# Cosformer attention into a GEGLU block on one core: another order for batch 0's opening, and batch 1's last 64 positions and a GpSimd copy in a later place

## The chip, the core and the metric

The kernel runs on one core of a Trainium2 chip. The core has a matrix engine (TensorE, PE in the profile; PEld is its loading of weights), a vector engine (VectorE, DVE), a scalar engine (ScalarE, ACT), GpSimd (POOL) and SyncE (SP), which here issues most of the DMA transfers. Each engine runs its instructions in the order in which the program issues them, and they wait for each other by semaphores. PSUM, the matrix engine's output memory, has eight banks of 512 fp32 columns for each of 128 partitions. The metric is the time of one execution on the device, in microseconds; lower is better.

## The reference

Eight batches of eight heads, 576 positions and 64 values per head go through a linear attention. Its result, as rows of 512 values, goes through a feed-forward block with a gate.

```python
batch, n_heads, seq, head_dim = (8, 8, 576, 64)
theta = pi / 2 * arange(S) / S
phi(x) = concatenate([relu(x) * cos(theta), relu(x) * sin(theta)], axis=-1)   # 64 -> 128 features
q_p, k_p = phi(q), phi(k)
kv  = einsum('bhsf,bhsd->bhfd', k_p, v)
z   = sum(k_p, axis=2)
num = einsum('bhsf,bhfd->bhsd', q_p, kv)
den = einsum('bhsf,bhf->bhs', q_p, z)[..., None] + 1e-06
x   = (num / den) as rows of tokens: 4608 x 512

g   = x @ w_gate                       # 512 x 1536
val = x @ w_val                        # 512 x 1536
out = (gelu(g) * val) @ w_out          # 1536 x 512
```

## The kernel before

**Attention.** The 576 positions of a batch lie in five tiles: tiles 0 to 3 have 128 positions, tile 4 the last 64. `load` (L76) brings a tensor of one batch in two DMAs, for the odd and the even partitions; `h0:h1` picks heads and `j0:j1` tiles. `sq` and `sk` (L351, L354) multiply one tile of q or k by cosine or sine and apply relu, on DVE (`"v"`) or ACT (`"s"`). `cast_v` (L140) casts heads of v to bf16, beside a column of ones. `kv_heads` (L152) multiplies keys by values, 5 matmuls a head, into one bank for four heads, and `kv_evac` (L166) copies that bank to SBUF; `kv_half` does both. q is turned either by PE (`q_by_pe`, L323, 8 transposes into a bank, with a copy `q_evac`, L331) or by a DMA on SP (`turn_q`, L144). `numer_mm` (L171) multiplies turned queries by kv, four matmuls for each group of four heads; `norm` (L180) adds epsilon (den), takes the reciprocal (rec) and multiplies (xb), all on DVE. The result, in one of four rotating buffers `xb`, is turned into `xT`, either by PE (`x_by_pe`, L339, with a copy) or by a DMA transpose on SP (`turn_x`, L204). For tile 4 that DMA writes a buffer `xr`, and a POOL copy (L212) brings 64 columns of it into `xT`.

**Feed-forward.** It runs in nine blocks: block 0 has the 576 tokens of batch 0, blocks 1 to 7 have 512 tokens each and block 8 has 448, so from block 1 on a block doesn't end where a batch does; the last 64 positions of batch 1 belong to block 2. A block has 12 units, one for each 128 columns of the 1536. In a unit, `gate` (L217) makes 4 matmuls into a bank and ACT applies Gelu into `gel`; `value` (L228) makes 4 matmuls into another bank, and DVE multiplies `gel` by it into `hT`. `o_part` (L259) makes 12 matmuls per 128 tokens for the output projection; ACT copies the bank to `o_sb`, and SP stores it. `hT` has two tiles, used by turns. Output tiles are aligned to 128 tokens of the whole sequence, so the last 64 tokens of a block go along with the next one: `carry(n)` (L245), one POOL copy of 12 x 64 columns from one `hT` to the first 64 columns of the other.

**Order.** All is written out by hand: instructions go to each engine in program order. `dummies` (L126) are matmuls on zeros whose results nobody reads.

- L86 to L103: loads of batch 0, on SP and one on ACT: k in two halves; q's first two tiles; v as heads 0 to 3, 4 and 5, 6 and 7; q's other tiles.
- L358 to L399: the opening: k scaled, q's tiles 0 and 1 scaled and turned by PE, v cast, kv made and copied, tiles 0 and 1 of the attention of batch 0. L363 and L398 are tiny copies that make POOL's weight loads (`load_w`, L307) wait: the first for q's first tiles, the other for x0.
- L413 to L448: block 0 by pieces. Its gates and values for units 0 to 5 are mixed with tiles 2, 3 and 4 of batch 0's attention. `Y(t, bank)` is the numerator and norm of tile t into that bank and the next; `X(t, bank, eng)` turns it into `xT`. `gv_unit(n, jt, c0, w, gb, vb, mid)` is a gate into bank gb, the steps of `mid`, then the value into bank vb; A is columns 0 to 255 and Bw 256 to 575.
- L451 to L456: q of batch 1 and w_out on POOL's queue; a tiny POOL copy (L454) that waits for a w_out load; behind it k and v of batch 1 on SP.
- L466 to L482: the rest of block 0's units; the table `between` puts q of batch 1 and, after unit 11, `carry(0)` among them.
- L483 to L522: k and v of batch 1, its kv, and tiles 0 to 3 of its attention, among the output tiles of block 0.
- From L524: `attn_step(b, i)`: for i = 0 the keys by values of batch b into banks 6 and 7, with copies; for i > 0 tile i-1 into `bank` and the next, turned by SP. `mid[n][jt]` holds steps that run between gate and value of unit jt of block n, `after[n][jt]` those that run behind the unit. For block 1, `attn_step(2, 0)` stands in `after[1][4]`, `attn_step(2, 1)` (banks 6 and 7) in `after[1][5]`, and `attn_step(2, 2)` (banks 4 and 5) in `mid[1][6]`. `attn_step(1, 5)`, batch 1's tile 4, stands in `mid[1][3]`.

Of the kernel before, what the change touches and what calls it, by code (L numbers as in the profile page):

```python
# [16 lines left out]
def kernel(  # L17
# [44 lines left out]
    vf = sb.tile([128, H, NJ + 1, D], FP32, name="vf")  # L62
# [13 lines left out]
    def load(dst, t, b, h0=0, h1=H, even=None, odd=None, j0=0, j1=NJ + 1):  # L76
        runs = t[b, h0:h1].rearrange("h (i r) d -> i h r d", r=9)
        for s, r0, n, eng in ((1, 5, 4, odd), (0, 0, 5, even)):
            n = min(n, j1)
            (eng or nc.sync).dma_start(  # L80
                out=dst[s:128:2, h0:h1, j0:n].rearrange("p h j d -> p h (j d)"),
                in_=runs[:, :, r0 + j0:r0 + n].rearrange("i h r d -> i h (r d)"),
            )
# [14 lines left out]
    nc.gpsimd.memset(vf[:, :, NJ], 0.0)  # L98
    load(qf, q, 0, j1=2)
    load(vf, v, 0, 0, 4)  # L100
    load(vf, v, 0, 4, 6)
    load(vf, v, 0, 6, 8)
    load(qf, q, 0, j0=2)  # L103

    nc.vector.tensor_scalar(par_i, par_i, 1, None, op0=ALU.bitwise_and)  # L105
# [20 lines left out]
    def dummies(n, bank=7):  # L126
        for _ in range(n):
            nc.tensor.matmul(ps[:, bank, :], lhsT=junk[:, 0:128], rhs=junk, start=True, stop=True)  # L128
# [11 lines left out]
    def cast_v(b, h0, h1, eng="v"):  # L140
        cp = nc.vector.tensor_copy if eng == "v" else nc.scalar.copy
        cp(vx[b % 2][:, :, h0:h1, 0:D], vf[:, h0:h1].rearrange("p h j d -> p j h d"))  # L142
# [6 lines left out]
        )  # L149


    def kv_heads(b, h0, h1, bank):  # L152
        for h in range(h0, h1):
            for j in range(NJ + 1):
                nc.tensor.matmul(  # L155
                    ps[:, bank, (h % 4) * (D + 1):(h % 4 + 1) * (D + 1)],
                    lhsT=kp[:, j, h, :],
                    rhs=vx[b % 2][:, j, h, 0:D + 1],
                    start=(j == 0), stop=(j == NJ),
                )  # L160

    def kv_half(b, g, bank, eng="s"):
        kv_heads(b, 4 * g, 4 * g + 4, bank)
        kv_evac(b, g, bank, eng)

    def kv_evac(b, g, bank, eng):  # L166
        src = ps[:, bank, 0:4 * (D + 1)].rearrange("p (h e) -> p h e", e=D + 1)
        dst = kv[b % 2][:, 4 * g:4 * g + 4, 0:D + 1]
        (nc.scalar.copy if eng == "s" else nc.vector.tensor_copy)(dst, src)

    def numer_mm(b, t, bank, g, rows=128):  # L171
        for h in range(4 * g, 4 * g + 4):
            nc.tensor.matmul(  # L173
                ps[0:rows, bank + g, (h % 4) * (D + 1):(h % 4 + 1) * (D + 1)],
                lhsT=qT[b % 2][:, t, h, 0:rows],
                rhs=kv[b % 2][:, h, 0:D + 1],
                start=True, stop=True,
            )

    def norm(xb, bank, g0, g1, rows=128):  # L180

        n = g1 - g0
        nd = ps[0:rows, bank + g0:bank + g1, 0:4 * (D + 1)].rearrange("p g (h e) -> p g h e", e=D + 1)
        den = rot.tile([128, 2, 4], FP32, name="den")
        nc.vector.tensor_scalar(den[0:rows, 0:n], nd[:, :, :, D], EPS, None, op0=ALU.add)  # L185
        rec = rot.tile([128, 2, 4], FP32, name="rec")
        nc.vector.reciprocal(rec[0:rows, 0:n], den[0:rows, 0:n])  # L187
        nc.vector.tensor_tensor(  # L188
            xb[0:rows, g0:g1], nd[:, :, :, 0:D],
            rec[0:rows, 0:n, :, None].to_broadcast([rows, n, 4, D]), op=ALU.mult,  # L190
        )
# [25 lines left out]
    def gate(n, jt, c0, w, gb):  # L217

        p0 = starts[n] + c0
        for ct in range(CT):  # L220
            nc.tensor.matmul(  # L221
                ps[:, gb, 0:w], lhsT=wg_sb[:, ct, jt * 128:(jt + 1) * 128],
                rhs=xT[:, ct, p0:p0 + w], start=(ct == 0), stop=(ct == CT - 1),
            )
        gels[n, jt, c0] = gel = rot.tile([128, 512], FP32, name="gel", bufs=4)
        nc.scalar.activation(gel[:, 0:w], ps[:, gb, 0:w], AF.Gelu)  # L226

    def value(n, jt, c0, w, vb):  # L228

        p0 = starts[n] + c0  # L230
        for ct in range(CT):
            nc.tensor.matmul(  # L232
                ps[:, vb, 0:w], lhsT=wv_sb[:, ct, jt * 128:(jt + 1) * 128],
                rhs=xT[:, ct, p0:p0 + w], start=(ct == 0), stop=(ct == CT - 1),
            )
        gel = gels.pop((n, jt, c0))
        nc.vector.tensor_mul(hT[n % 2][:, jt, 64 + c0:64 + c0 + w], gel[:, 0:w], ps[:, vb, 0:w])  # L237

    def gv_unit(n, jt, c0, w, gb, vb, mid=()):
        gate(n, jt, c0, w, gb)  # L240
        for f in mid:
            f()
        value(n, jt, c0, w, vb)
# [79 lines left out]
    def q_by_pe(b, j, bank, eng, h0=0, h1=H):  # L323

        qb = ps[:, bank, :].bitcast(BF16).rearrange("p (h t) -> p h t", h=H)
        for h in range(h0, h1):
            nc.tensor.transpose(out=qb[:, h, :], in_=qp[:, j, h, :], identity=ident)  # L327
        if eng is not None:
            q_evac(b, j, bank, eng, h0, h1)

    def q_evac(b, j, bank, eng, h0=0, h1=H):  # L331
        qb = ps[:, bank, :].bitcast(BF16).rearrange("p (h t) -> p h t", h=H)
        cp = nc.vector.tensor_copy if eng == "v" else nc.scalar.copy
        if j < NJ:
            cp(qT[b % 2][:, j, h0:h1], qb[:, h0:h1])
        else:
            cp(qT[b % 2][:, j, h0:h1, 0:64], qb[:, h0:h1, 0:128:2])

    def x_by_pe(b, t, xb, bank, eng, c0=0, c1=CT):  # L339
        p0 = b * S + t * 128  # L340
        cp = nc.vector.tensor_copy if eng == "v" else nc.scalar.copy
        xb2 = xb.rearrange("p g h d -> p (g h d)")
        rows = 128 if t < NJ else 64
        view = ps[:, bank, 0:256].bitcast(BF16).rearrange("p (c t) -> p c t", c=CT)
        for ct in range(c0, c1):
            nc.tensor.transpose(  # L346
                out=view[:, ct, 0:rows], in_=xb2[0:rows, ct * 128:(ct + 1) * 128], identity=ident[0:rows, 0:rows],
            )
        cp(xT[:, c0:c1, p0:p0 + rows], view[:, c0:c1, 0:rows])  # L349

    def sq(j, which, eng, *h):  # L351
        scale(Q, j, which, eng, *h)
# [11 lines left out]
    load_w(0, 2)  # L364
    load_w(2, 4)
    load_w(4, 8)
    sq(0, 0, "v"), sq(1, 1, "s"), sq(0, 1, "v"), sq(1, 0, "v")
    q_by_pe(0, 0, 0, None)
    q_by_pe(0, 1, 1, None)
    dummies(2)  # L370
    cast_v(0, 0, 2, "v")
    cast_v(0, 2, 4, "s")
    kv_heads(0, 0, 4, 4)
    q_evac(0, 0, 0, "v")
    q_evac(0, 1, 1, "s", 0, 4)
    cast_v(0, 4, 6, "v")
    cast_v(0, 6, 7, "v")
    kv_evac(0, 0, 4, "s")
    cast_v(0, 7, 8, "s")
    dummies(1)  # L380
    kv_heads(0, 4, 6, 5)
    x0, x1 = new_xb(), new_xb()
    numer_mm(0, 0, 6, 0)
    norm(x0, 6, 0, 1)
    kv_heads(0, 6, 8, 5)
    kv_evac(0, 1, 5, "s")
    q_evac(0, 1, 1, "s", 4, 8)
    dummies(1, 3)
    numer_mm(0, 0, 6, 1)
    norm(x0, 6, 1, 2)  # L390
    x_by_pe(0, 0, x0, 4, "s", 0, 2)
    sq(2, 0, "v"), sq(2, 1, "v")
    numer_mm(0, 1, 0, 0)
    numer_mm(0, 1, 0, 1)
    norm(x1, 0, 0, 2)
    x_by_pe(0, 0, x0, 4, "s", 2, 4)

    nc.gpsimd.tensor_copy(tiny[0:1, 1:2], x0[0:1, 1, 3, D - 1:D])  # L398
    load_w(8, 12)  # L399
# [2 lines left out]
    A, Bw = (0, 256), (256, 320)  # L402
    xs = {1: x1}

    def X(t, bank, eng):
        return lambda: x_by_pe(0, t, xs[t], bank, eng)

    def Y(t, bank):
        def f():
            xs[t] = numer(0, t, bank, 128 if t < NJ else 64)  # L410
        return f

    gate(0, 0, 0, 128, 5)  # L413
    gate(0, 1, 0, 128, 4)
    q_by_pe(0, 2, 3, None)
    X(1, 2, "s")()
    q_evac(0, 2, 3, "v")
    sq(3, 0, "v"), sq(3, 1, "s")
# [5 lines left out]
    value(0, 0, 128, 128, 2)  # L424
    value(0, 1, 128, 128, 3)
    q_by_pe(0, 3, 6, "s")
    X(2, 0, "v")()
    gate(0, 2, *A, 5)
    gate(0, 3, *A, 4)
    sq(4, 1, "s"), sq(4, 0, "v")  # L430
    gv_unit(0, 0, 256, 128, 1, 2)
    Y(3, 0)()
    value(0, 2, *A, 7)
    value(0, 3, *A, 3)
    q_by_pe(0, 4, 6, "s")
    gv_unit(0, 1, 256, 128, 5, 2, (X(3, 0, "s"),))
    Y(4, 3)()
    gv_unit(0, 0, 384, 128, 5, 1)
    gv_unit(0, 1, 384, 128, 6, 2)
    gate(0, 4, *A, 5)  # L440
    X(4, 7, "v")()
    gate(0, 5, *A, 0)
    gv_unit(0, 2, *Bw, 1, 6)
    gv_unit(0, 3, *Bw, 2, 7)
    value(0, 4, *A, 3)
    value(0, 5, *A, 4)
    gv_unit(0, 0, 512, 64, 5, 6)
    gv_unit(0, 1, 512, 64, 1, 7)  # L448


    load_q(1, nc.gpsimd)  # L451
# [7 lines left out]
    def L(f, *a):  # L459
        return lambda: f(*a)  # L460


    def T(t, bank, eng):
# [7 lines left out]
        (9, 0): (L(sq, 4, 0, "v"), L(sq, 4, 1, "s"), ),  # L471
        (9, 1): (L(turn_q, 1, 2, 5), ),
        (10, 1): (L(load_q, 2), ),
        (11, 1): (L(carry, 0), ),
    }
    for jt in range(4, 12):
        for i, (c0, w) in enumerate((A, Bw)):
# [55 lines left out]
    after = {n: {jt: [] for jt in range(JT)} for n in range(NB)}  # L533

    mid = {n: {jt: [] for jt in range(JT)} for n in range(NB)}
    mid[1][3].append(L(attn_step, 1, 5))
    for n in range(1, 7):
        b = n + 1
        a = after[n]
# [75 lines left out]
```

## Time and profile before

| what | us |
|---|---|
| time, median of 3 runs | 328.04 (327.54 to 328.16) |
| the profiled execution: time | 328.16 |
| the profiled execution: span from first to last instruction | 326.3 |
| PE busy, first 10 us (the 26 dummies) | 8.11 of 10 |
| PE busy, 10 to 15 / 15 to 20 / 20 to 25 / 25 to 30 us | 4.14 / 4.17 / 4.31 / 4.79 of 5 |
| PE busy in every 5 us from 30 to 130 us, but for 45 to 50 and 65 to 70 | 4.95 to 5.00 |
| PE busy, 45 to 50 / 65 to 70 us | 4.77 / 4.72 |
| mean granted TensorE clock | 0.996 |

A line of the view in order of time has the start, the duration, the engine, the line of the code, the operation, what is written and read with its shape, how many instructions are merged, and in brackets how long the engine idled before it and what it waited for. A line of the view of waits has the engine, what it was about to run, what released it, the total in us, how many times, and the longest. Matmul records overlap, since matmuls are pipelined; the distance from start to start is what one costs. A DMA is issued by a queue (SPq, ACTq, POOLq), and "landing" is the time from its issue until its data is there.

### The profile page before, as it was taken

How to read it: one execution, taken by the hardware profiler on the slowest of the kernel's cores; microseconds unless marked ns; L12 is line 12 of the kernel's file. 1: busy time of each engine (PE TensorE's matmuls, PEld its weight loads, DVE VectorE, ACT ScalarE, POOL GpSimd, SP SyncE). 2: the span in 40 equal slices, each digit the busy share in tenths (PEclk: the TensorE clock that was granted, in tenths of full speed). 3: DMA queues.
4: the chain of work that ended last, by engine and by line, in shares of the span. 5: the costliest groups of instructions: out<-in, count | busy, mean ns of one | idle time of the engine just before them, and what ended most of it. 6: DMA issues, size and time to landing. Idle time of an engine off the chain costs nothing.

```text
span 326.3 us, 5822 instructions
## 1 busy us (share of the span) xinstructions
PE 314.7 (96%) x2181; PEld 166.8 (51%) x2214; DVE 168.5 (52%) x381; ACT 150.9 (46%) x272; POOL 22.4 (7%) x43
## 2 busy tenths in 40 slices
PE   7789999999999999999999999999999999999993
PEld 3587866455445444554455445544554444445442
DVE  4885776678653675365736474537454232222200
ACT  5664664863483257425642475237522222323321
POOL 2741010000100010001000100010000100100000
PEclk9999999999999999999999999999999999999998
DMA  7999999998999929991999379986433111000124
GB/s 217 289 204 275 232 293 304 329 187 177 275 201 307 276 56 188 318 252 48 149 316 276 66 141 259 319 91 117 110 68 79 32 32 34 32 32 32 43 63 91
DMA packets 88332, 55.56 MB, mean 170 GB/s; under 512 B 53104, under 2 KB 83568, under 8 KB 88304
## 3 DMA queue, kind: packets, MB, share of 16 engines
q1 hardware_dynamic: 81776, 48.84, 61.4%
q0 software_dynamic: 6096, 5.90, 10.1%
q10 hardware_dynamic: 432, 0.46, 0.5%
q8 instruction: 17, 0.28, 0.4%
q14 instruction: 11, 0.09, 0.1%
HBM read 37.75 MB, written 9.44 MB: 145 GB/s over the span
## 4 chain that ended last, share of the span: by engine, by line
PE 90%; DVE 4%; DMA 2%; issue 1%; ACT 1%; POOL 0%; DVEq 0%; POOLq 0%; ACTq 0%
PE ps L232 28%; PE ps L221 28%; PE ps L262 26%; PE ps L155 3%; PE ps L173 3%; DMA kf<-in_k_dram 2%; DVE kp L136 2%; PE ps L280 1%; PE ps L327 1%; DVE xb L188 1%; DVE vx L142 1%; DVE qp L136 1%; PE ps L346 0%; DVE hT L237 0%; DVE rec L187 0%
## 5 line engine op out<-in xcount | busy, mean ns | idle before, releaser
L237 DVE TENSOR_TENSOR hT<-gel,ps 128x512 bf16<-128x512 f32 (+5 forms) x126 | 76.1, 608 | 93.7 <-PE ps L232 92.0
L221 PE MATMUL ps<-xT,wg_sb 128*128 128x512 bf16 (+5 forms) x491 | 111.6, 348 | 1.2 <-ACT xT L349 0.5
L232 PE MATMUL ps<-xT,wv_sb 128*128 128x512 bf16 (+5 forms) x497 | 111.8, 348 | 0.4
L226 ACT ACTIVATE gel<-ps 128x512 f32<-128x512 f32 (+5 forms) x126 | 67.3, 536 | 73.7 <-PE ps L221 49.0
L262 PE MATMUL ps<-wo_sb,hT 128*128 128x512 bf16 x408 | 94.1, 379 | 0.6
L221 PEld LDWEIGHTS <-wg_sb 128*128 128x128 bf16 x504 | 47.1, 98 | 45.2 <-issue 0.6
L232 PEld LDWEIGHTS <-wv_sb 128*128 128x128 bf16 x504 | 45.7, 98 | 39.0
L262 PEld LDWEIGHTS <-hT 128*128 128x128 bf16 x420 | 40.7, 98 | 47.8
L291 ACT COPY o_sb<-ps 128x512 f32<-128x512 f32 x35 | 20.5, 586 | 76.2 <-PE ps L262 75.1
L188 DVE TENSOR_TENSOR xb<-ps,rec 128x512 bf16<-128x512 f32 (+2 forms) x41 | 27.8, 678 | 1.6 <-DMA xr<-xb 0.2
L185 DVE TENSOR_SCALAR den<-ps 128x8 f32<-128x8 f32 (+2 forms) x41 | 6.7, 164 | 41.3 <-PE ps L173 41.1
L138 ACT ACTIVATE kp<-kf,sin_c 128x512 bf16<-128x512 f32 (+1 forms) x41 | 25.4, 681 | 0.9 <-DMA kf<-in_k_dram 0.9
L173 PEld LDWEIGHTS <-qT 128*128 128x128 bf16 (+1 forms) x320 | 15.3, 98 | 9.4 <-issue 1.3
L136 DVE TENSOR_SCALAR kp<-kf,cos_c 128x512 bf16<-128x512 f32 (+1 forms) x45 | 18.7, 463 | 1.5 <-DMA kf<-in_k_dram 1.5
L138 ACT ACTIVATE qp<-qf,sin_c 128x512 bf16<-128x512 f32 x26 | 17.9, 713 | 0.0
L173 PE MATMUL ps<-kv,qT 128*128 128x65 bf16 (+1 forms) x320 | 17.0, 194 | 0.9 <-ACT gel L226 0.7
L136 DVE TENSOR_SCALAR qp<-qf,cos_c 128x512 bf16<-128x512 f32 x40 | 17.6, 479 | 0.0
L212 POOL COPY xT<-xr 128x256 bf16<-128x256 bf16 x7 | 2.8, 402 | 199.2 <-DMA xr<-xb 199.2
L155 PEld LDWEIGHTS <-kp 128*128 128x128 bf16 x320 | 10.9, 97 | 2.8 <-issue 0.5
L155 PE MATMUL ps<-vx,kp 128*128 128x65 bf16 x320 | 11.3, 193 | 0.5 <-DVE xb L188 0.2
L128 PE MATMUL ps<-hT 128*128 128x512 bf16 x29 | 9.1, 476 | 1.7 <-DVE par_i L105 1.7
L142 ACT CAST vx<-vf 128x1280 bf16<-128x1280 f32 (+2 forms) x9 | 9.4, 1047 | 0.9 <-DMA vf<-in_v_dram 0.9
(54 smaller groups left out, 90.7 us busy)
## 6 DMA issues: line engine op xcount, KB each, us to landing
out_dram<-o_sb SPq DMA_DIRECT2D x38, 128.0 KB, 2.4
kf<-in_k_dram SPq DMA_DIRECT2D x7, 640.0 KB, 7.5
out_dram<-o_sb SPq DMA_DIRECT2D x16, 256.0 KB, 2.9
qf<-in_q_dram SPq DMA_DIRECT2D x6, 640.0 KB, 5.9
vf<-in_v_dram SPq DMA_DIRECT2D x6, 640.0 KB, 9.4
kf<-in_k_dram SPq DMA_DIRECT2D x7, 512.0 KB, 6.4
qf<-in_q_dram SPq DMA_DIRECT2D x6, 512.0 KB, 4.9
vf<-in_v_dram SPq DMA_DIRECT2D x6, 512.0 KB, 8.5
```

Source lines behind the costliest of these rows:

```text
L136: nc.vector.tensor_scalar(d, s, col, 0.0, op0=ALU.mult, op1=ALU.max)
L138: nc.scalar.activation(d, s, AF.Relu, scale=col)
L142: cp(vx[b % 2][:, :, h0:h1, 0:D], vf[:, h0:h1].rearrange("p h j d -> p j h d"))
L155: nc.tensor.matmul(ps[:, bank, (h % 4) * (D + 1):(h % 4 + 1) * (D + 1)], lhsT=kp[:, j, h, :], rhs=vx[b % 2][:, j, h, 0:D + 1], start=(j == ...
L173: nc.tensor.matmul(ps[0:rows, bank + g, (h % 4) * (D + 1):(h % 4 + 1) * (D + 1)], lhsT=qT[b % 2][:, t, h, 0:rows], rhs=kv[b % 2][:, h, 0:D ...
L188: nc.vector.tensor_tensor(xb[0:rows, g0:g1], nd[:, :, :, 0:D], rec[0:rows, 0:n, :, None].to_broadcast([rows, n, 4, D]), op=ALU.mult,)
L221: nc.tensor.matmul(ps[:, gb, 0:w], lhsT=wg_sb[:, ct, jt * 128:(jt + 1) * 128], rhs=xT[:, ct, p0:p0 + w], start=(ct == 0), stop=(ct == CT - 1),
L226: nc.scalar.activation(gel[:, 0:w], ps[:, gb, 0:w], AF.Gelu)
L232: nc.tensor.matmul(ps[:, vb, 0:w], lhsT=wv_sb[:, ct, jt * 128:(jt + 1) * 128], rhs=xT[:, ct, p0:p0 + w], start=(ct == 0), stop=(ct == CT - 1),
L237: nc.vector.tensor_mul(hT[n % 2][:, jt, 64 + c0:64 + c0 + w], gel[:, 0:w], ps[:, vb, 0:w])
L262: nc.tensor.matmul(ps[:, bank, :], lhsT=hT[n % 2][:, jt, c0:c0 + 128], rhs=wo_sb[:, jt, :], start=(jt == 0), stop=(jt == JT - 1),)
L291: nc.scalar.copy(o_sb, ps[:, bank, :])
```

## The change

Four things change.

1. v of batch 0 comes in two loads (heads 0 to 3 and 4 to 7), not three, so SP's queue has two DMAs fewer ahead of q's other tiles. Keys by values are again made by four heads at a time; `kv_half` can leave out the copy.
2. The opening. q's tiles 0 and 1 are scaled with cosine on DVE and sine on ACT, each tile followed by its transposes. The copies of the turned queries are whole ones on DVE. The copy of kv for heads 0 to 3 moves to DVE, behind the cast of heads 4 and 5, and the second cast on ACT has heads 6 and 7. The numerator of tile 0 follows all eight heads' keys by values. Behind the first transposes stand eight dummies instead of four, in other places. Of tile 2, the sine product is on ACT and only the cosine product on DVE, ahead of tile 1's norm; its transposes stand ahead of block 0's first gates.
3. Block 0's pieces: other banks throughout, and Y(3) between the values of units 2 and 3; unit 0's columns 256 to 383 come behind Y(3) and the transposes of tile 4.
4. `carry(0)` moves from the end of block 0 to `mid[1][5]`, and batch 1's tile 4 from `mid[1][3]` to just ahead of it, into banks 4 and 5.

```diff
-    load(vf, v, 0, 4, 6)
-    load(vf, v, 0, 6, 8)
+    load(vf, v, 0, 4, 8)
     load(qf, q, 0, j0=2)
...
-    def kv_heads(b, h0, h1, bank):
-        for h in range(h0, h1):
+    def kv_half(b, g, bank, eng="s"):
+        for h in range(4 * g, 4 * g + 4):
...
-    def kv_half(b, g, bank, eng="s"):
-        kv_heads(b, 4 * g, 4 * g + 4, bank)
-        kv_evac(b, g, bank, eng)
+        if eng is not None:
+            kv_evac(b, g, bank, eng)
...
     load_w(4, 8)
-    sq(0, 0, "v"), sq(1, 1, "s"), sq(0, 1, "v"), sq(1, 0, "v")
-    q_by_pe(0, 0, 0, None)
-    q_by_pe(0, 1, 1, None)
-    dummies(2)
+    for j in range(2):
+        sq(j, 0, "v"), sq(j, 1, "s")
+        q_by_pe(0, j, j, None)
+    dummies(3)
+    q_evac(0, 0, 0, "v")
     cast_v(0, 0, 2, "v")
     cast_v(0, 2, 4, "s")
-    kv_heads(0, 0, 4, 4)
-    q_evac(0, 0, 0, "v")
-    q_evac(0, 1, 1, "s", 0, 4)
+    kv_half(0, 0, 4, None)
+    q_evac(0, 1, 1, "v")
+    dummies(2)
     cast_v(0, 4, 6, "v")
-    cast_v(0, 6, 7, "v")
-    kv_evac(0, 0, 4, "s")
-    cast_v(0, 7, 8, "s")
-    dummies(1)
-    kv_heads(0, 4, 6, 5)
+    cast_v(0, 6, 8, "s")
+    kv_evac(0, 0, 4, "v")
+    kv_half(0, 1, 5, "s")
     x0, x1 = new_xb(), new_xb()
     numer_mm(0, 0, 6, 0)
     norm(x0, 6, 0, 1)
-    kv_heads(0, 6, 8, 5)
-    kv_evac(0, 1, 5, "s")
-    q_evac(0, 1, 1, "s", 4, 8)
-    dummies(1, 3)
+    dummies(1, 4)
     numer_mm(0, 0, 6, 1)
+    sq(2, 1, "s")
     norm(x0, 6, 1, 2)
-    x_by_pe(0, 0, x0, 4, "s", 0, 2)
-    sq(2, 0, "v"), sq(2, 1, "v")
+    sq(2, 0, "v")
     numer_mm(0, 1, 0, 0)
     numer_mm(0, 1, 0, 1)
     norm(x1, 0, 0, 2)
+    x_by_pe(0, 0, x0, 4, "s", 0, 2)
+    dummies(2, 5)
     x_by_pe(0, 0, x0, 4, "s", 2, 4)
+    q_by_pe(0, 2, 3, None)
...
     gate(0, 0, 0, 128, 5)
     gate(0, 1, 0, 128, 4)
-    q_by_pe(0, 2, 3, None)
     X(1, 2, "s")()
...
     q_by_pe(0, 3, 6, "s")
+    gate(0, 2, *A, 5)
     X(2, 0, "v")()
-    gate(0, 2, *A, 5)
+    sq(4, 1, "s"), sq(4, 0, "v")
     gate(0, 3, *A, 4)
-    sq(4, 1, "s"), sq(4, 0, "v")
-    gv_unit(0, 0, 256, 128, 1, 2)
+    value(0, 2, *A, 7)
     Y(3, 0)()
-    value(0, 2, *A, 7)
-    value(0, 3, *A, 3)
-    q_by_pe(0, 4, 6, "s")
-    gv_unit(0, 1, 256, 128, 5, 2, (X(3, 0, "s"),))
-    Y(4, 3)()
+    value(0, 3, *A, 2)
+    q_by_pe(0, 4, 3, "s")
+    gv_unit(0, 0, 256, 128, 5, 6)
+    gv_unit(0, 1, 256, 128, 4, 7, (X(3, 0, "s"),))
+    Y(4, 2)()
     gv_unit(0, 0, 384, 128, 5, 1)
-    gv_unit(0, 1, 384, 128, 6, 2)
+    gv_unit(0, 1, 384, 128, 4, 0)
     gate(0, 4, *A, 5)
     X(4, 7, "v")()
-    gate(0, 5, *A, 0)
-    gv_unit(0, 2, *Bw, 1, 6)
-    gv_unit(0, 3, *Bw, 2, 7)
-    value(0, 4, *A, 3)
-    value(0, 5, *A, 4)
-    gv_unit(0, 0, 512, 64, 5, 6)
-    gv_unit(0, 1, 512, 64, 1, 7)
+    gate(0, 5, *A, 4)
+    gv_unit(0, 2, *Bw, 2, 6)
+    gv_unit(0, 3, *Bw, 3, 7)
+    value(0, 4, *A, 1)
+    value(0, 5, *A, 2)
+    gv_unit(0, 0, 512, 64, 4, 6)
+    gv_unit(0, 1, 512, 64, 5, 7)
...
         (10, 1): (L(load_q, 2), ),
-        (11, 1): (L(carry, 0), ),
     }
...
-    mid[1][3].append(L(attn_step, 1, 5))
+    mid[1][5].append(L(attn_step, 1, 5, 4))
+
+    mid[1][5].append(L(carry, 0))
     for n in range(1, 7):
```

## The prediction

> **What bounds the kernel now.** I read the busy shares first, then the chain of waits, then PE's own waits, then the instructions in order of time where PE waited.
>
> ```profile
> span 326.3 us, 5822 instructions
> PE 314.7 (96%) x2181; PEld 166.8 (51%) x2214; DVE 168.5 (52%) x381; ACT 150.9 (46%) x272; POOL 22.4 (7%) x43
> ...
> PE 90%; DVE 4%; DMA 2%; issue 1%; ACT 1%; POOL 0%; DVEq 0%; POOLq 0%; ACTq 0%
> ```
>
> PE is 90% of the chain that ends last. So an edit is worth the PE idle time that it adds or removes, as far as no later wait takes it back. PE's waits in the first 90 us (line, releaser, total us, times, longest):
>
> ```profile
> PE ps L327 <- DVE qp L136: 0.7, 1, 0.7
> PE ps L173 <- ACT gel L226: 0.7, 1, 0.7
> PE ps L221 <- ACT xT L349: 0.5, 2, 0.3
> PE ps L346 <- DVE xb L188: 0.4, 1, 0.4
> PE ps L173 <- ACT kv L169: 0.2, 1, 0.2
> PE ps L155 <- DVE xb L188: 0.2, 1, 0.2
> PE ps L155 <- DVE vx L142: 0.2, 1, 0.2
> ```
>
> All of them lie where the diff works. In order of time (start, duration, engine, line):
>
> ```profile
> 22.00 0.28 ACT L226 ACTIVATE gel<-ps 128x128 f32<-128x128 f32 x1
> 22.33 0.29 PE L173 MATMUL ps<-kv,qT 128*128 128x65 bf16 x4 [0.68 <-ACT gel L226]
> ...
> 24.62 0.59 ACT L349 COPY xT<-ps 128x512 bf16<-128x512 bf16 x1
> 25.27 0.38 PE L221 MATMUL ps<-xT,wg_sb 128*128 128x128 bf16 x4 [0.21 <-ACT xT L349]
> ```
> ```profile
> 46.52 1.01 POOL L248 COPY hT<-hT 128x768 bf16<-128x768 bf16 x1 [10.44 <-DVE hT L237]
> ```
> ```profile
> 68.04 0.69 DVE L188 TENSOR_TENSOR xb<-ps,rec 128x512 bf16<-128x512 f32 x1
> 68.79 1.37 PE L155 MATMUL ps<-vx,kp 128*128 128x65 bf16 x40 [0.23 <-DVE xb L188]
> 77.77 0.40 POOL L212 COPY xT<-xr 128x256 bf16<-128x256 bf16 x1 [30.24 <-DMA xr<-xb]
> ```
>
> The reader should see three places. At 22 us the second half of Y(3)'s numerator sits behind a Gelu that still reads bank 1. At 25.27 block 0's gates wait for the xT copy of tile 3. At 68.79 batch 2's keys by values wait for the normalisation of batch 1's last 64 positions, because both use banks 6 and 7.
>
> **Part 1, the opening.** I lay the new order out with spacings from these rows: sq on DVE 0.40, on ACT 0.61; cast of two heads 0.48 (done after 0.56); q_evac of 1024 columns 0.60 on DVE, 0.91 on ACT; eight transposes 0.45; 20 key-value matmuls 0.61 (30 and a filler take 1.12 at 11.92); a filler 0.22; norm of two groups 1.12 from den to xb's end; a reader starts about 0.2 after a matmul group's last start.
> The first queries are split over DVE and ACT, so tile 0 is ready at 10.12 (9.40+0.72) and PE starts at 10.18, not 10.56. Tile 1 is turned at 10.80 after ACT's second sq. DVE: q_evac(0) 10.83, cast 11.42, q_evac(1) 11.90, cast of heads 4 and 5 12.49, kv_evac 12.97 to 13.40. PE: heads 0 to 3 from 12.03, two fillers to 13.07, heads 4 to 7 from 13.10 to 13.71, numerator at once. Before, those heads also ended at about 13.7, and ACT's kv_evac began at 13.85; now 13.88.
> The second load of v is two DMAs fewer on SP's queue, and those issue at 0.6 to 0.75 each, so q's rest is issued some 1.4 earlier. Heads 4 and 5 now wait for all of heads 4 to 7. Before, the last of those landed at 7.6+4.9=12.5; the same bytes are queued no later now, so the cast at 12.49 waits nothing. That is the upper value; the lower bound is a landing 1 us later, for which DVE has no cover.
> Group 1's norm then runs 14.80 to 15.63 (before to 15.44), but only one sq, not two, stands ahead of x1's norm, so x1 is ready at 17.06 instead of 17.26. q_by_pe(2) now precedes the gates; gates and transposes together end at 16.97 (before 17.02). X(1), values, Y(2), the second pair of gates and q_by_pe(3) follow 0.25 earlier, PE done at 19.48 instead of 19.73. Weights cover this: the first gate weights land at 9.80+5.8=15.6, the next pair at 18.3 and 19.7, ahead of 16.53, 19.48 and 20.59. The four more fillers (8 for 4, 0.22 each) fall into waits for DVE and ACT.
> Then the order matters. Y(3) uses banks 0 and 1, and no Gelu is left in bank 1. PE: gate(2) 19.48, X(2) 19.92, gate(3) 20.15, value(2) 20.59, Y(3) 21.03 (qT ready 20.69), value(3), q_by_pe(4) 21.71, unit 0 at 256 22.16, gate 22.60, X(3) 22.82 (x3 ready 22.67), value, Y(4) to 23.52. ACT's xT copy of tile 3 ends at 23.86, after q_evac(4) and two Gelus; gate(0) at 384 starts 23.91 where it started 25.27. PE waits 0.4 there. From that point all is PE-bound in both. **Opening: -1.36**; with v a microsecond late, -0.4.
>
> **Part 2, what is left of it at batch 1's keys by values.** Block 0 would end 1.36 earlier; L262 would start at 44.33, not 45.69. But k of batch 1 is issued at 36.10, after the POOL cast of line 454 that waits for a w_out load; the DMA share is 1.08 to 1.41 in every 5 us from 15 to 45, so this does not move. (q of batch 1, landed at 22.40+11.7=34.1, stays ahead of its first sq, then at 35.92-1.36=34.56.) Its even rows land at 36.8+8.2=45.0. ACT's sin products start then, four by 0.61 to 47.49, the o_sb copy 0.49, the fifth product to 48.70 (before 49.69). PE could start at 44.33+18x0.216=48.22 and needs the fifth product at about 48.35; it loses 0.35 to 0.4.
> DVE gains here. One of its five cosine products took 1049 ns beside a median of 475 while POOL's carry ran at 46.52; without that copy its first cast ends at about 47.98, not 49.87. Before, PE waited about 0.34 here (49.92 less 45.69+18x0.216=49.58). Nothing else queued on DVE waits for carry. So: -1.36 -0.34 +0.4 = **-1.3 after batch 1**; nothing handed back would give -1.65.
>
> **Part 3, the last 64 positions.** Batch 1's numerator (8 matmuls, 0.25), den, rec, xb (1.12 on DVE) and one DMA transpose on SP move past the keys by values and two units. PE before: value(4) ends 67.53+0.86=68.39, L155 starts at 68.79 (the bracket says 0.23, since a matmul's record runs about 0.16 past its stream) and its stream ends at 70.0; 40 of them take 1.21 elsewhere (99.05), here 1.37. After, the casts (DVE, and ACT to 67.01 in shifted time) are done before PE gets to the heads that use them, so **-0.40** goes. The 0.25 is only moved. The norm now falls where DVE idled 2.06 (before 71.99). On SP the transpose still follows q of batch 3, issued 69.57 to 71.16; xb is ready at about 70.6, so SP holds nothing up. Queued behind xr's copy on POOL there is now carry, needed by no one until block 1's first output tile near 86.9.
> k of batch 2 lands at 51.6+8.5=60.1, ahead of its sk at 62.99-1.3=61.7. The next thing late is xb of batch 2's tile 3: it takes the buffer that this transpose reads, and waited 0.16 for it at 77.8. xr landed at 77.7 behind q's load, and that doesn't move with PE. So DVE will wait up to 1.7 there, and its product of unit 8 ends at about 79.1 as before; PE wants that bank at 80.75-1.67=79.08. Cost 0 to 0.15; I take 0.05.
>
> The sum: -1.3 -0.40 +0.05 = -1.65. Against the profiled execution (span 326.3, time 328.16) this is 326.5. That execution is 0.12 above the median of three, 328.04, less than I can resolve; I leave **326.5**.
>
> **A page against a row.** At carry's new place, 78.2 to 79.0, DVE has den, rec, xb and hT. The xb product at 77.81 ran beside POOL's copy of 77.77 in 691 ns, its usual time, so by the row the new place costs nothing. The Trainium skill, "SBUF — State Buffer", section "Who interferes with whom", says that copies, casts and tensor_scalar in two-port modes lock a pair of ports with GpSimd and that the second to issue blocks fully. By the rule a small tensor_scalar or reciprocal caught by carry could hold DVE for up to 0.83, which the bank at 79.08 would pass on to PE: 327.3. I keep the row's sum.
>
> **Rivals.** (a) The lead is lost before batch 1's keys by values: v lands late (opening -0.4), or k's landing sets a later start than I count. For it: k is tied to DMA. Against it: ACT's fifth product was 1.0 earlier even with the wait. Then 328.16-0.34-0.40=327.4. (b) Slower: carry writes 64 columns of hT of block 1 and now ends near 79.0, behind the xr copy. If block 1's products into that tile had to wait for it, unit 5's product, due at about 70.6, would stop DVE; PE would run out at value(7), which needs the bank, at 75.07-1.67=73.4, and go on at about 79.7. That is 6.3 more: 332.8. It decides if the wait ends later than 73.4. Against it: while tile 0 of batch 2 was being written into xT by a DMA (73.74 to 78.2), gates reading other columns of xT started at 75.93 and 77.91 unheld, so strided parts of one tile are kept apart. (c) Nothing is handed back at 45 us: 326.1.
>
> **How the numbers follow.** About 0.66 us (0.2%) is what a measurement can tell here, so 327.4 is the line. Forecast 0.58 (own range 326.2 to 327.0), (c) 0.07, (a) 0.20, (b) or another new stall 0.15. Half of (a) lies under the line: faster 0.58+0.07+0.10=0.75, same 0.11 and slower 0.14. The range 325.9 to 327.7 leaves out (b) and the ends.
>
> **What would show it.** PE's wait of 0.68 on a Gelu at Y(3) gone; first 128-column gate of tile 3 near 23.9; no cosine product over 0.5 us near 45 to 47; L155 of batch 1 starting near 48.2 with a wait on ACT kp; L155 of batch 2 with no wait, 1.7 earlier than 68.79; xb of tile 3 waiting about 1.7 for xr. I am wrong if the tile 3 gate starts after 24.8, if DVE waits on vf at 12.5, or if hT waits for POOL in block 1.

## The result and the profile after

The changed kernel takes 326.04 us (median of four runs, 325.82 to 326.12) against 327.8 (four runs, 327.54 to 328.16): ratio 0.9944, interval 0.9927 to 0.9962, 1.76 us less. Forecast were 326.5 us and a gain of 1.65. The time lies inside the range of 325.9 to 327.7, but below the narrower 326.2 to 327.0 that the forecast gave itself: it was counted from one execution of 328.16, and 1.65 from the median of 327.8 would have been 326.15.

The page of the changed kernel, its span, its busy times and the shares of its chain of waits:

```profile
span 324.3 us, 5829 instructions
...
PE 315.1 (97%) x2185; PEld 167.1 (52%) x2218; DVE 168.0 (52%) x380; ACT 151.3 (47%) x271; POOL 21.7 (7%) x43
...
PE 93%; DMA 2%; SPq 1%; DVE 1%; issue 1%; POOL 0%; ACT 0%; POOLq 0%; DVEq 0%
```

PE's part of the chain went from 90% to 93%, and DVE's from 4% to 1%. The list of waits for the first 90 us keeps only two lines for PE (columns as in the prediction):

```profile
PE ps L127 <- DVE par_i L104: 1.7, 1, 1.7
...
PE ps L324 <- ACT qp L137: 0.6, 1, 0.6
```

The first stands at the start-up fillers (the 26 dummies) and is there before too. The second is the first of the seven in another form: the transposes of queries still wait for the scaled queries, 0.55 where it was 0.70, and now for ACT. The other six are gone from the list; PE still idles about 0.28 ahead of tile 3's first gate, which the list does not show, and some waits of the opening lie under fillers (see "No fillers"). All lines of the new kernel lie one to three lower: gate L218, value L229, numerator L170, keys by values L154, output L259, normalisation L185, carry L245. The same places in order of time (start, duration, engine, line). The opening:

```profile
12.78 0.73 ACT L141 CAST vx<-vf 128x640 bf16<-128x640 f32 x1 [0.96 <-DMA vf<-in_v_dram]
...
21.40 0.42 PE L170 MATMUL ps<-kv,qT 128*128 128x65 bf16 x8
...
23.64 0.58 ACT L346 COPY xT<-ps 128x512 bf16<-128x512 bf16 x1
...
24.27 0.38 PE L218 MATMUL ps<-xT,wg_sb 128*128 128x128 bf16 x4
```

Y(3)'s numerator is one group of eight without a wait where it was broken by 0.68. Tile 3's first gate is at 24.27 instead of 25.27, still right behind the copy of tile 3 into xT. But ACT waits 0.96 for v. Batch 1's keys by values, before:

```profile
45.69 4.05 PE L262 MATMUL ps<-wo_sb,hT 128*128 128x512 bf16 x17
...
49.92 1.36 PE L155 MATMUL ps<-vx,kp 128*128 128x65 bf16 x40 [0.18 <-DVE vx L142]
```

And after:

```profile
44.70 4.05 PE L259 MATMUL ps<-wo_sb,hT 128*128 128x512 bf16 x17
48.59 1.43 PE L154 MATMUL ps<-vx,kp 128*128 128x65 bf16 x40
...
44.69 2.55 ACT L137 ACTIVATE kp<-kf,sin_c 128x512 bf16<-128x512 f32 x4
47.98 0.72 ACT L137 ACTIVATE kp<-kf,sin_c 128x512 bf16<-128x512 f32 x1
```

From the output products to the keys by values are 3.89 us, the own time of 18 matmuls (18 x 0.216; one is missing from the records), where there were 4.23. ACT waits for no transfer. Batch 2's keys by values and the norm behind them:

```profile
66.87 1.37 PE L154 MATMUL ps<-vx,kp 128*128 128x65 bf16 x40
...
77.36 0.69 DVE L185 TENSOR_TENSOR xb<-ps,rec 128x512 bf16<-128x512 f32 x1 [1.37 <-DMA xr<-xb]
...
77.66 0.82 POOL L245 COPY hT<-hT 128x768 bf16<-128x768 bf16 x1
```

The wait of 0.23 is gone, the wait for xr has grown from 0.16 to 1.37, and the carry runs beside DVE's products xb and hT, which take 0.69 and 0.68 as elsewhere.

Where the time came from, as the lead of PE's stream over the kernel before:

| place | before | after | lead |
|---|---|---|---|
| tile 3's first gate | 25.27 | 24.27 | 1.00 |
| output products ahead of batch 1's keys by values | 45.69 | 44.70 | 0.99 |
| first recorded output product behind them | 51.34 | 50.07 | 1.27 |
| value product behind batch 2's keys by values | 70.85 | 69.19 | 1.66 |
| last matmul ends | 321.31 | 319.65 | 1.66 |

The spans differ by 2.0. The other 0.34 lies behind the last instruction: from the end of the last copy (321.92 and 320.26) to the end of the span it is 4.38 before and 4.04 after. In the twelve experiments below it lies between 3.65 and 4.46, so 0.3 of a span or of a single time says nothing about an edit.

### The profile page after: what moved, and what is told of

It reads as the page before. It is cut to its first block, busy times and chain, and to the rows that moved or that the text cites. A ratio compares the mean times of both kernels' runs of the same rounds, so it can differ in the third digit from the quotient of the medians.

```text
span 324.3 us, 5829 instructions
## 1 busy us (share of the span) xinstructions
PE 315.1 (97%) x2185; PEld 167.1 (52%) x2218; DVE 168.0 (52%) x380; ACT 151.3 (47%) x271; POOL 21.7 (7%) x43
## 4 chain that ended last, share of the span: by engine, by line
PE 93%; DMA 2%; SPq 1%; DVE 1%; issue 1%; POOL 0%; ACT 0%; POOLq 0%; DVEq 0%
PE ps L218 29%; PE ps L229 29%; PE ps L259 28%; PE ps L170 3%; PE ps L154 3%; DMA vf<-in_v_dram 2%; SPq L80 1%; PE ps L277 1%; PE ps L324 1%; PE ps L343 1%; DVE vx L141 0%; ACT xT L346 0%; DVE qp L135 0%; POOL vf L98 0%; POOL qf L97 0%
## 5 line engine op out<-in xcount | busy, mean ns | idle before, releaser
L218 PE MATMUL ps<-xT,wg_sb 128*128 128x512 bf16 (+5 forms) x492 | 111.8, 348 | 0.7
L229 PE MATMUL ps<-xT,wv_sb 128*128 128x512 bf16 (+5 forms) x496 | 111.8, 348 | 0.4
L259 PE MATMUL ps<-wo_sb,hT 128*128 128x512 bf16 x408 | 94.3, 379 | 0.6
L218 PEld LDWEIGHTS <-wg_sb 128*128 128x128 bf16 x504 | 47.1, 98 | 44.5
L229 PEld LDWEIGHTS <-wv_sb 128*128 128x128 bf16 x504 | 45.7, 98 | 39.0
L259 PEld LDWEIGHTS <-hT 128*128 128x128 bf16 x420 | 40.8, 98 | 47.7
L185 DVE TENSOR_TENSOR xb<-ps,rec 128x512 bf16<-128x512 f32 (+2 forms) x41 | 27.8, 678 | 2.8 <-DMA xr<-xb 1.4
L170 PEld LDWEIGHTS <-qT 128*128 128x128 bf16 (+1 forms) x320 | 15.1, 98 | 8.3 <-issue 0.4
L137 ACT ACTIVATE qp<-qf,sin_c 128x512 bf16<-128x512 f32 x28 | 19.3, 713 | 0.1
L170 PE MATMUL ps<-kv,qT 128*128 128x65 bf16 (+1 forms) x320 | 16.6, 194 | 0.1
L154 PEld LDWEIGHTS <-kp 128*128 128x128 bf16 x320 | 10.9, 97 | 2.6 <-issue 0.7
L127 PE MATMUL ps<-hT 128*128 128x512 bf16 x33 | 10.2, 460 | 1.8 <-DVE par_i L104 1.7
L154 PE MATMUL ps<-vx,kp 128*128 128x65 bf16 x320 | 11.2, 193 | 0.1
L141 ACT CAST vx<-vf 128x1280 bf16<-128x1280 f32 (+1 forms) x9 | 9.7, 1076 | 1.2 <-DMA vf<-in_v_dram 1.2
```

The costliest lines, as they stand in the source:

```text
L137: nc.scalar.activation(d, s, AF.Relu, scale=col)
L154: nc.tensor.matmul(ps[:, bank, (h % 4) * (D + 1):(h % 4 + 1) * (D + 1)], lhsT=kp[:, j, h, :], rhs=vx[b % 2][:, j, h, 0:D + 1], start=(j == ...
L170: nc.tensor.matmul(ps[0:rows, bank + g, (h % 4) * (D + 1):(h % 4 + 1) * (D + 1)], lhsT=qT[b % 2][:, t, h, 0:rows], rhs=kv[b % 2][:, h, 0:D ...
L185: nc.vector.tensor_tensor(xb[0:rows, g0:g1], nd[:, :, :, 0:D], rec[0:rows, 0:n, :, None].to_broadcast([rows, n, 4, D]), op=ALU.mult,)
L218: nc.tensor.matmul(ps[:, gb, 0:w], lhsT=wg_sb[:, ct, jt * 128:(jt + 1) * 128], rhs=xT[:, ct, p0:p0 + w], start=(ct == 0), stop=(ct == CT - 1),
L229: nc.tensor.matmul(ps[:, vb, 0:w], lhsT=wv_sb[:, ct, jt * 128:(jt + 1) * 128], rhs=xT[:, ct, p0:p0 + w], start=(ct == 0), stop=(ct == CT - 1),
```

## The experiments

Times are medians in us, beside the kernel before on the same chip: 327.80 in the first group (the first four below), 327.81 in the second (the next four), 327.69 in the third (the last four).

**The late part alone.** The kernel before with only the last two edits:

```diff
-        (11, 1): (L(carry, 0), ),
-    mid[1][3].append(L(attn_step, 1, 5))
+    mid[1][5].append(L(attn_step, 1, 5, 4))
+    mid[1][5].append(L(carry, 0))
```

> The kernel before with only the late part: batch 1's last 64 positions behind batch 2's keys by values, in banks 4 and 5, and GpSimd's copy behind it. My theory: 0.34 us at batch 1's keys by values (DVE's slow product under GpSimd's copy) and 0.40 at batch 2's, 0.74 in all, so about 327.1 beside 327.8. Rival: ACT's fifth sine product holds batch 1's keys by values as much as DVE's cast did, so only 0.40 to 0.50 comes. Rival: these waits are covered by later ones, nothing.

Measured: 327.13 (326.97 to 327.60), ratio 0.9979, interval 0.9971 to 0.9988: 0.67 less. Output products at 45.48 and keys by values at 49.36, 3.88 apart; batch 2's start at 67.65 with no wait. The last copy starts 0.88 earlier (320.75 against 321.63), and 0.21 of that was there ahead of the output products, from an earlier start; 0.67 is left, as in the time. The terms of 0.34 and 0.40 hold, but for 0.06 of the first that is lost again in the keys by values.

**The opening alone.** The changed kernel with those two edits put back:

```diff
+        (11, 1): (L(carry, 0), ),
-    mid[1][5].append(L(attn_step, 1, 5, 4))
-    mid[1][5].append(L(carry, 0))
+    mid[1][3].append(L(attn_step, 1, 5))
```

> The changed kernel with the late part put back to where it was, so only v's loads, the opening and the order and banks of block 0's pieces. My theory: the gates of tile 3 start about 1.0 us earlier than in the kernel before (24.27 there in the changed kernel, 25.27 before) and none of it is handed back at batch 1's keys by values: about 326.8. Rival, as I had forecast it: k of batch 1 is tied to the transfers and 0.4 is handed back: about 327.2. The time of GpSimd's little copy of line 454 or 449, which lets k's load go, tells: 35.9 if tied, 35.0 if it moves.

Measured: 326.56 (326.36 to 326.79), ratio 0.9962, interval 0.9950 to 0.9974: 1.24 less. Both late waits are back, 0.18 at 48.69 and 0.23 at 67.56. The little copy ran at 35.50, between the two times of the expectation, and decides nothing; ACT did not wait for k. The two halves, 0.67 and 1.24, add up to 1.91 against 1.76 for the whole, which their intervals can't tell apart.

**The pieces alone.** In what follows "the front" is the opening up to the transposes of query tile 3, q_by_pe(3), and "the pieces" are what follows it in block 0. Here the loads and the front are those of before, and only the order and banks of the pieces, from q_by_pe(3) to the units at columns 512 on, are new:

```diff
+    gate(0, 2, *A, 5)
     X(2, 0, "v")()
-    gate(0, 2, *A, 5)
...
-    gv_unit(0, 0, 256, 128, 1, 2)
+    value(0, 2, *A, 7)
     Y(3, 0)()
...
```

> The kernel before with only the order and the banks of block 0's pieces from the transposes of query tile 3 on; loads, opening and late part as before. My theory: all of the opening's gain comes from here (no Gelu left in bank 1 ahead of Y(3)): 1.1 us, 326.7, and PE's wait of 0.68 gone; the new front of the opening is worth nothing or costs 0.1. Rival, as I had forecast it: 0.25 of the gain is from the front, so this run gets 0.1 to 0.3 less than the run with the whole opening. GpSimd's little copy of line 454: 35.9 if its move came with the loads of v and q or with DVE's pauses in the front, 35.0 if it follows PE's or ACT's progress.

Measured: 326.29 (325.80 to 326.86), ratio 0.9953, interval 0.9941 to 0.9965: 1.5 less, no less than the whole opening. The first weight load's issue on POOL follows q's landing, and so marks the start. Before:

```profile
9.80 1.41 POOL L308 DMA_DIRECT2D wg_sb<-in_moe_w_gate_dram  x1 [7.06 <-ACT wg_sb L363]
```

In this run, the issue and tile 3's first gate:

```profile
9.88 1.22 POOL L308 DMA_DIRECT2D wg_sb<-in_moe_w_gate_dram  x1 [7.15 <-ACT wg_sb L363]
```
```profile
24.25 0.38 PE L221 MATMUL ps<-xT,wg_sb 128*128 128x128 bf16 x4
```

That issue is made anywhere from 8.93 to 9.92 in these profiles, so the gate is best read from it. Before, and in the two experiments that keep its opening, the gate stands 15.47, 15.48 and 15.48 behind the issue. With the new pieces behind the old front: 14.37. The changed kernel itself: 24.27-9.92=14.35. Counted so, the pieces give 1.1 and the new front nothing.

**The banks alone.** The kernel before with one argument more, the carry and the place unchanged:

```diff
-    mid[1][3].append(L(attn_step, 1, 5))
+    mid[1][3].append(L(attn_step, 1, 5, 4))
```

> The kernel before with one word changed: batch 1's last 64 positions stay where they were, but use banks 4 and 5 and not 6 and 7. My theory: the wait of batch 2's keys by values is one for the bank, so 0.40 us comes without any move: 327.4, first matmul of line 155 of batch 2 at about 68.4. Rival: the order on DVE (casts, then the norm) or ACT's cast sets it, and nothing comes: 327.8.

Measured: 327.36 (326.97 to 329.81), ratio 0.9995, interval 0.9981 to 1.001: with one of eleven runs at 329.81 (the others end at 327.65), the time settles nothing. The trace does:

```profile
67.89 1.37 PE L155 MATMUL ps<-vx,kp 128*128 128x65 bf16 x40
```

The value product before it starts at 67.02 and takes 0.86, so PE goes on at once, and the bracket of 0.23 is gone. The lead over the kernel before is 0.51 at the output products (45.18), from an earlier start, and 0.90 at the last copy (320.73): 0.39 came here and stayed. It was the bank that PE waited for; moving the step was not needed for that.

**v in three loads again.** The changed kernel with the loads of before:

```diff
-    load(vf, v, 0, 4, 8)
+    load(vf, v, 0, 4, 6)
+    load(vf, v, 0, 6, 8)
```

> The changed kernel with v of batch 0 loaded as 4, 2 and 2 heads again; its casts and all else as changed. My theory: in the changed kernel the cast of heads 4 and 5 waited for the landing of all of heads 4 to 7 (it began at 12.80, DVE was free at about 12.63), so this gives back 0.1 to 0.2: 325.9 beside 326.0, and no wait of DVE for vf ahead of the second cast. Rival: the cast is held by its engine, not by the load, and the two DMAs more on SP's queue cost nothing either: no difference. Rival: this load alone makes the new front as fast as the old: 0.3.

Measured: 325.88 (325.44 to 326.11), ratio 0.9935, interval 0.9922 to 0.9947, not told apart from the changed kernel. DVE's cast of heads 4 and 5 runs without a wait for v, as expected, but ACT still waits 0.93 for the last heads, and the gate stands 14.67 behind the issue. PE was behind here from the first transposes on: they began at 10.21, without a wait behind the start-up fillers and 0.70 behind the issue, where the changed kernel has 0.37. So the landing of v is not all that holds the front. The merge of the two loads is worth nothing that shows.

**The carry back.** The changed kernel with the carry at block 0's end:

```diff
+        (11, 1): (L(carry, 0), ),
-    mid[1][5].append(L(carry, 0))
```

> The changed kernel with GpSimd's copy of block 0's last columns back at the end of block 0. My theory: one of DVE's five cosine products of k takes 1.05 us again, its cast ends 0.57 later, and batch 1's keys by values start 0.34 later behind the output matmuls (4.23 instead of 3.89 after their start): 0.3 slower than the changed kernel, 326.35. Rival: ACT's fifth sine product, which ends at 48.70, holds PE anyway, and only 0.1 is lost.

Measured: 326.04 (325.89 to 326.54), ratio 0.9945, interval 0.9932 to 0.9959: in time the same as the changed kernel. In the trace, all instructions of the cosine product near 45 us, for this kernel and then for the changed one (duration in ns min/median/max, first and last start in us):

```profile
L135 DVE TENSOR_SCALAR kp<-kf,cos_c x5: 473/475/1051, 45.2 to 47.4; 128x512 bf16<-128x512 f32 x5
```
```profile
L135 DVE TENSOR_SCALAR kp<-kf,cos_c x5: 481/481/481, 45.4 to 47.0; 128x512 bf16<-128x512 f32 x5
```

With the copy on POOL (45.38, 1.01 us) one of five takes 0.58 longer; keys by values then start 4.23 behind the output products, and the first output product behind them 5.65, as before, instead of 5.37. The carry's part is 0.28 of PE's time, less than these times resolve.

**The old front with everything else new.** Loads and front of before, new pieces, new late part:

```diff
+    load(vf, v, 0, 4, 6)
+    load(vf, v, 0, 6, 8)
-    load(vf, v, 0, 4, 8)
...
+    sq(0, 0, "v"), sq(1, 1, "s"), sq(0, 1, "v"), sq(1, 0, "v")
-    for j in range(2):
-        sq(j, 0, "v"), sq(j, 1, "s")
...
```

> The kernel before with the new order and banks of block 0's pieces and the late part, but with the old loads of v and the old front of the opening. My theory: the new front gains nothing (the first transposes wait for the 26 dummies, and v's second load comes late), so this is as fast as the changed kernel or 0.1 to 0.3 faster: 325.7 to 326.0. Rival, as forecast: the new front is worth 0.25, so this is 0.25 slower: 326.3.

Measured: 325.53 (325.34 to 325.74), ratio 0.9928, interval 0.9915 to 0.9940. It is 2.28 under the kernel before and 0.4 to 0.5 under the changed one, none of whose nine runs (four at the result, five further below, 325.76 to 326.12) is as low; the two ratios' intervals overlap. Tile 3's gate is at 23.67, 14.38 behind the issue at 9.29, so the new front saves nothing. That it costs time is suggested by the times and not shown: 0.60 of lead over the changed kernel's first profile is there at the gate, and nearly all of that is the earlier landing of q (0.63); 0.41 of it reaches the last copy, and another 0.39 lies behind it.

**A larger lead.** The same, with gate(4) ahead of the units at 384, which fills PE's wait of 0.28 for the xT copy of tile 3:

```diff
+    gate(0, 4, *A, 5)
+    gv_unit(0, 0, 384, 128, 4, 1)
+    gv_unit(0, 1, 384, 128, 6, 0)
-    gv_unit(0, 0, 384, 128, 5, 1)
-    gv_unit(0, 1, 384, 128, 4, 0)
-    gate(0, 4, *A, 5)
...
+    value(0, 4, *A, 1)
...
-    value(0, 4, *A, 1)
```

> As the run before it, and the gate of unit 4 for columns 0 to 255 is put ahead of the gates of columns 384 to 511, where PE still waited 0.28 for the copy of tile 3 into xT (its value goes ahead of the third part of units 2 and 3, so that no fifth Gelu buffer is needed). My theory: that wait is filled and 0.28 comes: 325.5. Rival: the Gelu of the moved gate delays ACT's copy of tile 3, or the weights of units 4 to 7 (landed at about 24.7 before) hold the value, and nothing comes or it gets slower.

Measured: 325.55 (325.03 to 325.70), ratio 0.9926, interval 0.9913 to 0.9938: no gain over the one before it. Counted from the issue at 9.53, the output products stand 0.10 nearer (44.24, 34.71 behind it, where the run before has 44.10 and 34.81). But batch 1's keys and values then hold the engines up:

```profile
44.87 2.56 ACT L138 ACTIVATE kp<-kf,sin_c 128x512 bf16<-128x512 f32 x4 [0.53 <-DMA kf<-in_k_dram]
```
```profile
48.08 0.56 DVE L142 CAST vx<-vf 128x640 bf16<-128x640 f32 x1 [0.23 <-DMA vf<-in_v_dram]
```
```profile
48.59 1.26 PE L155 MATMUL ps<-vx,kp 128*128 128x65 bf16 x36 [0.17 <-ACT kp L138]
```

PE begins at 48.13, stops after four and goes on at 48.59. This is the hand-back of the prediction: of a lead of 0.46 over the changed kernel at the output products, 0.17 is left at the first recorded one behind the keys by values (49.90 against 50.07). The run before has it too: ACT waited 0.44 for k there, and a lead of 0.60 shrank to 0.41.

**Keys issued earlier.** The same, with the copy that holds k's issue reading q of batch 1 in place of w_out:

```diff
-    nc.gpsimd.tensor_copy(kf[0:2, 0, 0, 0:1], wo_sb[0:2, 2, C - 1:C])
+    nc.gpsimd.tensor_copy(kf[0:2, 0, 0, 0:1], qf[0:2, H - 1, NJ - 1, D - 1:D])
```

> The run with the gate of unit 4 moved, and GpSimd's little copy that lets batch 1's k load go reads q of batch 1 and not a part of w_out. In that run ACT waited 0.53 for k and DVE 0.23 for v of batch 1, and PE 0.2 for ACT's fifth sine product. My theory: k is issued some 1.5 us earlier, these waits go, and the filled wait at 24 us is kept: 0.2 to 0.3 faster than that run, 325.3. Rival: k and v then share the DMA engines with w_out, which lands late for the output matmuls, and nothing comes or it gets slower.

Measured: 325.49 (325.35 to 326.03), ratio 0.9934, interval 0.9922 to 0.9947. Nothing gained. DVE waited 0.23 for v, PE 0.37 for ACT's last product at 48.71, and ACT for k:

```profile
45.00 2.56 ACT L138 ACTIVATE kp<-kf,sin_c 128x512 bf16<-128x512 f32 x4 [0.73 <-DMA kf<-in_k_dram]
```

k was issued at 33.98 instead of 35.85 and ACT began at 45.00 instead of 44.87: an earlier issue brought no earlier landing. The Trainium skill, "DMA: Bandwidth & Descriptors", section "Issuing engines are not separate DMA queues", has it that transfers end up on the same 16 DMA engines and interleave there, whichever engine starts them; the unmoved landing agrees with that, but which transfers k shared them with was not separated.

**The changed kernel once more**, unchanged, to see how far it scatters.

> The changed kernel itself, on the same chip as the three that follow: about 326.0 beside 327.8. The profile's start of the first weight load (9.92 in its first profile, 9.27 to 9.88 in the others) and of the little copy of line 449 tell how much two profiles of one kernel differ before PE is the bound.

Measured: 325.94 (325.76 to 326.00), ratio 0.9943, interval 0.9929 to 0.9957. In its profile q landed almost 1 us earlier than in the first, and this is what came of it:

```profile
8.93 0.95 POOL L305 DMA_DIRECT2D wg_sb<-in_moe_w_gate_dram  x1 [6.20 <-ACT wg_sb L360]
...
10.64 0.69 DVE L332 COPY qT<-ps 128x1024 bf16<-128x1024 bf16 x1 [1.08 <-PE ps L324]
...
11.78 0.73 ACT L141 CAST vx<-vf 128x640 bf16<-128x640 f32 x1 [0.93 <-DMA vf<-in_v_dram]
...
13.29 0.76 PE L154 MATMUL ps<-vx,kp 128*128 128x65 bf16 x20 [0.24 <-DVE vx L141]
...
24.09 0.38 PE L218 MATMUL ps<-xT,wg_sb 128*128 128x128 bf16 x4
```

The issue is 0.99 earlier than in the first, the gate only 0.18: 15.16 apart instead of 14.35. Over all kernels with the new front, gate less issue is 14.35, 14.35, 14.39, 14.41, 14.67, 14.67 and 15.16. When q landed this early the new front could not use it. Here the transposes began at 9.99, behind the start-up fillers; DVE waited 1.08 for them, since its order puts the copies of qT ahead of the casts of v, and PE then waited 0.24 for DVE's last cast at 13.29. The old front casts first, at 10.48 in the earliest of its profiles, and needs no transpose for that: with the issue at 9.27 its gate stood the usual 15.48 behind. An issue as early as 8.93 was not seen with it.

**One more buffer.** The changed kernel with a fifth xb, so that the norm does not wait for the transfer out of the fourth (xr is cut to one buffer):

```diff
-        return rot.tile([128, 2, 4, D], BF16, name="xb", bufs=4)
+        return rot.tile([128, 2, 4, D], BF16, name="xb", bufs=5)
-            xr = rot.tile([128, CT, 128], BF16, name="xr")
+            xr = rot.tile([128, CT, 128], BF16, name="xr", bufs=1)
```

> The changed kernel with five buffers for xb and one for xr. My theory: the wait of 1.37 us that DVE has for xr's transpose, ahead of the product xb of batch 2's tile 3, goes, and no time comes of it, since PE never waited for what lies behind: same as the changed kernel within 0.1. Rival: that wait is what PE would meet next, and 0.1 to 0.2 comes.

Measured: 325.53 (325.50 to 325.67), ratio 0.9933, interval 0.9921 to 0.9946, and 0.4 below the changed kernel beside it, against my theory of no difference. DVE's wait is gone: the same product starts at 75.72 without one, where the changed kernel beside it has

```profile
76.90 0.69 DVE L185 TENSOR_TENSOR xb<-ps,rec 128x512 bf16<-128x512 f32 x1 [1.10 <-DMA xr<-xb]
```

But PE never felt that wait: neither trace has a wait of PE from 66 to 89 us. Of the 0.4 between the two spans (323.7 and 324.1), 0.13 is there when the last copy starts (319.66 and 319.79); 0.12 of that is there already at the first recorded output product behind batch 1's keys by values (49.76 and 49.88), before the fifth buffer matters. The rest lies behind the last copy, in the stretch that differs from profile to profile. So where the 0.4 of the medians comes from stays open; the wait for xr is not shown as its cause.

**No fillers.** The changed kernel without eight of the opening's filler products, which no one reads:

```diff
-    dummies(3)
-    dummies(2)
-    dummies(1, 4)
-    dummies(2, 5)
```

> The changed kernel without the eight dummy matmuls behind the first transposes. My theory: they lie in PE's waits for DVE and ACT and cost nothing: same within 0.1. Rival: they hold PE back by up to 0.2 each time DVE is ready first, and it gets faster by 0.2 to 0.4. Rival: without them the granted clock falls in the opening and it gets slower by 0.3 or more, to be seen in the mean time of the matmuls from 10 to 20 us.

Measured: 326.15 (325.86 to 326.94), ratio 0.9954, interval 0.9942 to 0.9967: not told apart from the changed kernel. PE's waits of 1.2, 0.5, 0.3 and 0.3 stand where the fillers lay, the gate is 14.35 behind the issue, and the granted clock is 0.999 with them and without. Here they neither cost nor bring anything that these runs can tell.

## Why the prediction was right, and where its sizes were off

The mechanisms of the three gains were right, and so was the sum: 1.65 forecast, 1.66 at the last matmul, 1.76 in the time. Two of its terms were off, the opening by 0.36 and the hand-back by 0.4. That they cancel so closely is luck.

- **The opening, 1.36 forecast, 1.00 measured.** The step that failed is the one on the front, "0.25 earlier". 0.12 of the missing 0.36 is the start: the issue was at 9.92 and not at 9.80, and that q lands up to 1 us apart from profile to profile was not in the sum at all. The rest is the front itself. The forecast had heads 4 and 5 cast at 12.49 without a wait, on a landing of v at 12.5. DVE was free for them at about 12.63; the halves of v that ACT casts landed at about 12.75, DVE's cast ran at 12.80, x1 was ready at 17.40, not 17.06, and q_by_pe(3) started at 19.42 against 19.28 before: counted from the issue, where it was. The forecast had named a wait for vf at 12.5 as a sign of being wrong. Nor would an earlier v have been enough: in three profiles (issue at 8.93, 9.36 and 9.51) DVE's cast did not wait for v, the transposes followed the start-up fillers at once, and the gate was no nearer to the issue (15.16, 14.67 and 14.67 behind). The pieces were sized right: 1.1 forecast (1.36 less 0.25), 1.1 measured from the issue.
- **The hand-back at 45 us, 0.4 forecast, none in this profile.** Keys by values started at 48.59 without a wait, not near 48.2 with one for ACT. The forecast took k's issue as one time, fixed by transfers. It scatters: the little copy that releases it ran at 35.90, 35.23 and 35.01 with the opening of before, and at 35.85, 34.90 and 35.65 with PE 1.1 earlier, so it does not follow PE. In the changed kernel's profile it ran at 35.02, the even rows of k landed at 35.9+8.5=44.4 and not at 45.0, and the lead was smaller by 0.36, so ACT, which came to them at 44.69, was never held. With more lead, the sine product waits as described.
- **The carry and the bank, 0.34 and 0.40.** The carry gave 0.34 up to the keys by values' start, of which 0.28 was left behind them; the bank gave 0.39 from there (1.66-1.27). Both right, and each shown by itself in the trace; the times alone resolve neither.
- **The wait for xr, 0.05.** Forecast up to 1.7 on DVE and nearly nothing on PE; measured 1.37, since xr landed at 77.3 and not at 77.7, and none.
- **The page against the row.** The Trainium skill, "SBUF — State Buffer", section "Who interferes with whom", describes an exclusive lock between GpSimd and DVE's two-port operations. The cosine product of 1051 ns beside 475 agrees with it. The forecast's 327.3 went further than that section: it names no reciprocal among these operations, and that the small tensor_scalar, which reads PSUM, is one of them was assumed. At the carry's new place it cost nothing, but the trace does not try the rule there: the carry ran from 77.66 to 78.48 beside two products that read PSUM, and the small tensor_scalar began after it, at 78.56.
- **The rivals.** The slow one falls: block 1's products into hT ran at 70.44, 73.11 and 74.74, long before the carry, and DVE waited nowhere there for POOL. That the lead is lost at the front holds for the front's 0.25 alone. The case of nothing handed back is what this profile shows, with a smaller opening.
- **Two slips in its sums, neither in the 1.65.** Nothing handed back gives -1.36-0.34=-1.70, not -1.65. And rival (a) names an opening of -0.4, but its 327.4 counts none of it; with it, it would be 327.0.

## What to carry to other kernels

Ask of each wait which buffer or bank it is for before moving work: the larger two of the three gains here came from the banks and the order of a few pieces, and the rebuilt front, the largest part of the diff, gave nothing. A part of a kernel that starts when a transfer lands has to be read from that landing, not from the clock of the page. A gain ahead of a transfer that does not move with it is worth something only up to that transfer.

## What the runs showed of the hardware

- GpSimd's copy of SBUF to SBUF held one DVE product from SBUF for up to 0.58 us (1046 to 1051 ns for 474 or 475) in the five profiles where the carry lay at block 0's end, and left products that read PSUM at 0.69 and 0.68. The changed kernel has such a case too, which PE does not feel: a later carry at 118.11 took 1.02 us instead of 0.83, and the cosine product of q beside it 1043 ns instead of 479.
- The same program's first weight load was issued at 8.93 and at 9.92 us in two profiles, since q landed 1 us apart; the stretch behind the last instruction took 3.65 to 4.46.
- That issue takes POOL 1.20 to 1.41 us in kernels with the old front, where three of DVE's products lie beside it, and 0.89 to 0.95 with the new one, where there are two. No run tried that by itself.
